# Output products and memory products as 32-row tiles, with score visits between, in a hand-ordered attention and feed-forward kernel

## The chip, the cores and the metric

The kernel runs on one core of a Trainium2 chip. The metric is the device time of one execution in microseconds (us); lower is better. A core has five engines that matter here: TensorE (PE) multiplies matrices into eight banks of PSUM, VectorE (DVE) and ScalarE (ACT) read the banks and write SBUF, GpSimd (POOL) works on SBUF alone, and SyncE (SP) issues nearly all transfers. Each engine runs its own list of instructions in order and waits on semaphores for the others.

## The reference, cut to what matters

```python
q, k, v = heads(x @ wq), heads(x @ wk), heads(x @ wv)      # 2048 tokens, D = 512, 32 heads of 16, N = 4 segments of 512
for s in range(4):                                         # one segment after the other
    p = softmax(q[s] @ k[s].T * scale + mask)              # causal inside the segment
    a_dot = p @ v[s]
    a_mem = (phi(q[s]) @ M) / (phi(q[s]) @ z + 1e-6)       # memory of the earlier segments
    o[s] = sigmoid(beta) * a_mem + (1 - sigmoid(beta)) * a_dot
    M += phi(k[s]).T @ v[s];  z += phi(k[s]).sum(tokens)
a = o @ wo
b = (relu(x @ W_gate) * (x @ W_up)) @ W_down               # F = 1792
out = g * a + (1 - g) * b                                  # g = sigmoid((x * gate_w).sum(-1))
```

Everything is bf16 in memory; `B_x` is not used.

## The kernel before, in words

All weights are loaded once and stay in SBUF, and the four segments of 512 tokens are worked through in turn. For each segment there are these stages, all issued on PE:

- **Projections** (`proj`): 12 column blocks of q, k and v, each of 4 matmuls of 128x128 by 512 columns.
- **Score visits** (`visit`, names `quad...`): the 32 heads of 16 are laid out so that four blocks of scores are made at once by matmuls on four 32-row tiles of the array (`tile_position=(32j, 0)`), one PSUM bank for each. A visit of four banks is followed by one exponential on ACT over 2048 columns (line 714). In segments 1 to 3 `SEVEN` joins seven quads into four visits of seven blocks each (four banks and three banks, two exponentials). The first segment has 18 visits, the other three 15 each: 63.
- **Masks** on POOL (line 723), and **pv** (`flush`, names `pv...`): probabilities by values, on tiles of 64 rows by 32 columns, one for each of 4 groups of heads, followed on DVE and POOL by a chain (transposes, reciprocal, products) that ends in `oT`, the attention's share of the output product.
- **Memory** (`mu`, names `mu...`, on tiles of 64 columns) and **`nd`**: for each of 4 token tiles a product `num` (4 matmuls of 128x128 by 136 columns, of which only the blocks on the diagonal are not zero), then on DVE denominators, a reciprocal and a scaled product, and a transposing DMA into `amemT`.
- **Feed-forward** (`ffn`): 14 blocks of gate and up products, relu and a product into `hT`.
- **Output products** (`outp`, names `ob...`, `oo...`): for each of the 4 token tiles 14 matmuls with `W_down` (line 876) and 4 with `wo` (line 869) add up in one bank; `fin` scales the bank into `osb` on DVE (line 884) or ACT (line 885) and `st` stores it. `between` issues `outp` and `nd` of segment s-1 and s after the first visit of segment s, so they share the time with the visits of segment s.

A PE operation is in one of four modes, by the shape of its tiles: `f` (whole array: projections, feed-forward, output products, num), `r` (32 rows: visits), `h` (pv) and `c` (mu).

Which operation comes when is not decided by the loops. `program` numbers every operation as it adds it; `ORDER` holds, for each engine, the full list of these numbers in the order in which the engine executes them, and `BANKS` one digit for each use of PSUM (an `Epoch`), its first bank. `Sched` turns both into instructions and semaphore waits: an operation waits for what it reads, for the readers of what it overwrites, and for the readers of the bank's last holder. A PE operation is usually two matmuls of one accumulation, and operations of different stages alternate.

Numbered in this way, PE's list of before changes mode 145 times. Around the output products of segment 0, for example, it reads (a bar for each change of mode, xN for N operations in a row):

```
quad | pv | proj, ob x3 | quad (7 blocks) | ob, oo x10 | quad (7) | ob, oo x8 | quad (7) | ob, oo x8 | quad (7) | ob, oo x3, num, ffn, proj, num, ffn | quad ...
```

Of the kernel before, what the change touches and what calls it, by code (L numbers as in the profile page):

```python
# [47 lines left out]
1485 1486 1487 1488""",  # L48
    "act": """
# [892 lines left out]
```

## Time and profile before

| what | value |
|---|---|
| time, three runs | 261.5, 261.03 and 261.54 us; median 261.5 us |
| span of the profiled execution (first to last instruction) | 260.0 us; about 1.5 us of the time lies outside it |
| PE busy | 252.7 us (97% of the span) |
| ACT, DVE, POOL busy | 188.0, 171.7, 121.2 us (72%, 66%, 47%) |
| granted TensorE clock | 1.000 |

The profiled execution's own time is not listed apart from the three runs, so the span and the median stand side by side. In a line of instructions or of the timeline the first number is the start in us from the span's start and the second how long the group lasted; `x4` counts instructions. The ends of matmuls are modelled, so that successive matmuls overlap in the records: what counts is the distance from start to start. A few matmul records are missing, which shows as a gap of 0.16 us "issue" or a count one short.

### The profile page before, as it was taken

The numbers are of one execution on the slowest core, as the hardware profiler recorded it, in microseconds if no ns is written. First come the engines' busy times: TensorE is split into PE (matmuls) and PEld (weight loads), VectorE is DVE, ScalarE is ACT, GpSimd is POOL, SyncE is SP. The second block draws the span as 40 slices with busy tenths as digits, with TensorE's granted clock in tenths as the row PEclk, the third lists the DMA queues.
The fourth block names the chain that finished last, engine by engine and source line by source line (L and its number), as shares of the span: only waits on it lengthen the run. The fifth ranks groups of instructions, "written<-read, shape, count | busy, mean of one in ns | idle before, by whom it ended". The sixth has DMA issues, their size and how long they took to land.

```text
span 260.0 us, 6414 instructions
## 1 busy us (share of the span) xinstructions
PE 252.7 (97%) x2621; PEld 115.4 (44%) x2655; DVE 171.7 (66%) x342; ACT 188.0 (72%) x173; POOL 121.2 (47%) x295
## 2 busy tenths in 40 slices
PE   8999999999999999999999999999999999999997
PEld 4433443434444544444544444434444445343544
DVE  2487788778655789777834478677762138875764
ACT  4598898988778788987777666979787685787000
POOL 2014766575736372587402944257620881168100
DMA  6899997115362311422041023100023022100002
GB/s 217 244 297 221 204 171 162 59 61 143 69 151 52 64 26 37 84 42 63 3 126 42 3 42 59 28 0 0 4 45 83 15 28 43 40 4 0 3 3 81
DMA packets 34925, 19.61 MB, mean 75 GB/s; under 512 B 24144, under 2 KB 34256, under 8 KB 34896
## 3 DMA queue, kind: packets, MB, share of 16 engines
q1 hardware_dynamic: 34512, 18.80, 31.5%
q8 instruction: 21, 0.34, 0.6%
q10 hardware_dynamic: 384, 0.40, 0.4%
q14 instruction: 8, 0.07, 0.1%
HBM read 10.14 MB, written 2.11 MB: 47 GB/s over the span
## 4 chain that ended last, share of the span: by engine, by line
PE 97%; issue 2%; DVE 0%
PE ps L839 38%; PE ps L876 19%; PE ps L589 11%; PE ps L703 9%; PE ps L753 7%; PE ps L587 5%; PE ps L869 5%; PE ps L646 1%; PE ps L506 1%; PE ps L629 1%; PE ps L518 0%; PE ps L527 0%; DVE osb L884 0%
## 5 line engine op out<-in xcount | busy, mean ns | idle before, releaser
L714 ACT ACTIVATE E<-ps 128x2048 bf16<-128x2048 f32 (+1 forms) x75 | 134.3, 1808 | 35.0 <-PE ps L703 34.9
L723 POOL TENSOR_SCALAR_AFFINE_SELECT E<-E 128x256 bf16<-128x256 bf16 (+1 forms) x256 | 100.9, 422 | 103.7 <-ACT E L714 90.3
L839 PE MATMUL ps<-xT,wg 128*128 128x512 bf16 x216 | 58.7, 380 | 1.1 <-issue 0.6
L839 PE MATMUL ps<-xT,wu 128*128 128x512 bf16 x213 | 57.4, 380 | 1.6 <-issue 1.6
L876 PE MATMUL ps<-wd,hT 128*128 128x512 bf16 (+2 forms) x231 | 52.7, 366 | 0.9 <-issue 0.8
L850 DVE TENSOR_TENSOR hT<-ps,rl 128x512 bf16<-128x512 f32 x56 | 37.9, 681 | 14.7 <-PE ps L839 14.2
L876 PEld LDWEIGHTS ps<-wd,hT 128*128 128x128 bf16 x238 | 21.7, 98 | 25.0 <-issue 2.5
L839 PEld LDWEIGHTS ps<-xT,wu 128*128 128x128 bf16 x224 | 20.0, 98 | 25.5 <-issue 3.9
L839 PEld LDWEIGHTS ps<-xT,wg 128*128 128x128 bf16 x224 | 20.2, 98 | 24.5 <-issue 2.8
L884 DVE TENSOR_SCALAR osb<-ps,omg 128x512 bf16<-128x512 f32 (+2 forms) x15 | 10.6, 715 | 27.9 <-PE ps L869 23.9
L703 PE MATMUL ps<-qT,kp 32*128 32x512 bf16 (+7 forms) x512 | 27.6, 286 | 0.0
L761 DVE STREAM_TRANSPOSE Tn<-ps 128x512 f32<-128x512 f32 x32 | 21.4, 699 | 8.3 <-PE ps L753 8.2
L848 DVE TENSOR_SCALAR rl<-ps 128x512 bf16<-128x512 f32 x27 | 18.3, 684 | 9.3 <-PE ps L839 9.2
L847 ACT ACTIVATE rl<-ps 128x512 bf16<-128x512 f32 x29 | 17.1, 595 | 6.7 <-PE ps L839 6.7
L703 PEld LDWEIGHTS ps<-qT,kp 32*128 32x128 bf16 x512 | 9.1, 92 | 24.9 <-ACT E L714 9.3
L753 PE MATMUL ps<-E,vaug 64*17 64x128 bf16 (+7 forms) x512 | 18.6, 283 | 0.0
L753 PE MATMUL ps<-E,vsh 64*17 64x128 bf16 (+7 forms) x512 | 18.2, 283 | 0.0
L770 POOL TENSOR_TENSOR adT<-Tn,rdg 128x512 bf16<-128x512 f32 x12 | 12.7, 1055 | 11.7 <-DVE rdg L768 8.8
L587 PE MATMUL ps<-wv,xT 128*128 128x512 bf16 x60 | 16.6, 379 | 0.6 <-issue 0.6
L589 PE MATMUL ps<-xT,wk 128*128 128x512 bf16 x62 | 16.8, 379 | 0.1
L869 PE MATMUL ps<-wo,oT 128*128 128x512 bf16 (+2 forms) x67 | 16.1, 366 | 0.1
L589 PE MATMUL ps<-xT,wq 128*128 128x512 bf16 (+2 forms) x67 | 15.9, 367 | 0.2 <-issue 0.2
(70 smaller groups left out, 215.8 us busy)
## 6 DMA issues: line engine op xcount, KB each, us to landing
vsh<-vaug SPq DMA_DIRECT2D x8, 272.0 KB, 3.2
out_dram<-osb SPq DMA_DIRECT2D x15, 128.0 KB, 1.9
wg<-in_B_W_gate_dram SPq DMA_DIRECT2D x8, 224.0 KB, 6.1
wu<-in_B_W_up_dram SPq DMA_DIRECT2D x8, 224.0 KB, 5.2
osb<-in_A_x_dram SPq DMA_DIRECT2D x14, 128.0 KB, 3.0
wd<-in_B_W_down_dram SPq DMA_DIRECT2D x7, 256.0 KB, 3.4
wk<-in_A_wk_dram SPq DMA_DIRECT2D x4, 128.0 KB, 3.6
wv<-in_A_wv_dram SPq DMA_DIRECT2D x4, 128.0 KB, 3.6
```

Of the source, the lines that this page charges most:

```text
L587: ins = e.matmul(A(ep)[:, :], lhsT=V.xT[:, kt, tok + col * 128:tok + (col + 1) * 128], rhs=w[:, kt, :], start=(kt == 0), stop=(kt == KT - 1))
L589: ins = e.matmul(A(ep)[:, c0:c1], lhsT=w[:, kt, col * 128:(col + 1) * 128], rhs=V.xT[:, kt, tok + c0:tok + c1], start=(kt == 0 and c0 == 0 ...
L703: ins = q.matmul(PS[:, ep.bank + i, o:o + w], lhsT=V.kp[r, kslot(s, G), c, :], rhs=V.qT[r, qslot(s, G), q0:q0 + w], start=True, stop=True, ...
L714: return a.activation(V.E[:, n * 512:(n + k) * 512].rearrange("q (b n) -> q b n", n=512), PS[:, x.bank:x.bank + k, :], ACT.Exp, scale=SCALE)
L723: pool(lambda g, ap=ap, lim=lim: g.affine_select(out=ap, in_=ap, compare_op=ALU.is_ge, fill=0.0, base=lim, pattern=[[0, 4], [1, 64]], chan ...
L753: ins = q.matmul(A(eps[p])[32 * jj:32 * jj + 17, 64 * (c + u):64 * (c + u + n)], lhsT=v[:, 8 * G + 2 * jj + p, :], rhs=V.E[r, f:f + 64 * n ...
L761: dve(lambda e, p=p, ep=eps[p]: e.transpose(V.Tn[:, 2 * (G % (TNN // 2)) + p, :], A(ep)[:, :]), 709, writes=[f"Tn{2 * (G % (TNN // 2)) + p ...
L839: ins = e.matmul(A(ep)[:, :], lhsT=w[:, kt, f * 128:(f + 1) * 128], rhs=V.xT[:, kt, c % XR * 512:(c % XR + 1) * 512], start=(kt == 0), sto ...
L848: ("dve", lambda e, ep=eg, r=r: e.tensor_scalar(V.rl[:, r, :], A(ep)[:, :], 0.0, None, ALU.max), t_dve(512))],
L850: dve(lambda e, ep=eu, r=r, hs=hs: e.tensor_tensor(V.hT[:, hs, :], A(ep)[:, :], V.rl[:, r, :], ALU.mult), t_dve(512), reads=[f"rl{r}"], wr ...
L869: ins = e.matmul(A(ep)[:, 0:c1 - c0], lhsT=V.oT[:, ot[G], i * 128:(i + 1) * 128], rhs=V.wo[:, G, c0:c1], start=st_ and G == 0, stop=sp_ an ...
L876: ins = e.matmul(A(ep)[:, 0:c1 - c0], lhsT=V.hT[:, slots[f], i * 128:(i + 1) * 128], rhs=V.wd[:, f, c0:c1], start=st_ and f == f0, stop=sp ...
```

## The change

- `outp` of segments 0 to 2 becomes `outr`. Every 128x128 matmul by 512 columns is cut into four of 32 rows. One operation is two rows of the contraction times four token tiles, 8 matmuls on four tiles of the array, each into its own bank. There are four phases `p`; in a phase token tile i uses row tile (i+p)%4, and the phases run over all 18 blocks of the contraction. So four banks are held from the first to the last operation of a segment's output products, and all four sums end with the last one. The first operation of phases 1 to 3 waits for PE's own last operation of the phase before. There are 36 operations for each segment, in mode `r`. Segment 3 keeps the old form.
- `nd` takes two token tiles at once: one `num` of 32 matmuls of 32x128 by 34 columns (only the blocks that aren't zero), mode `r`, over four banks; DVE then does two `nde`, one `ndr` and one new `ndg` for both tiles and two `ndm`.
- `SEVEN` is empty: all visits have four banks, 72 visits instead of 63, 72 exponentials instead of 75.
- The cost that the planner holds for `gate` and its list of names `PORT` change; they issue no instruction.
- `ORDER` and `BANKS` are new for all engines.

Numbered in the same way, the new list changes mode 139 times. 19 of the 72 visits stand inside the runs of output products, and of the six `num` one does (at the end of the run in segment 3). The runs read, with their banks:

```
segment 0's products: ob x2, quad, ob x5, quad, ob x6, quad, ob x5, quad, ob x9, quad, ob x5, quad, ob x4, quad | ffn (bank 5, after fin0_1) ...
segment 1's products: ob x3, quad, ob x5, quad, ob x5, quad, ob x5, quad, ob x9, quad, ob x5, quad, ob x4, quad | proj (bank 5, after fin1_0) ...
segment 2's products: ob x3, quad, ob x5, quad, ob x5, quad, ob x5, quad, ob x8, quad, ob x5, quad, ob x5, num | ffn (bank 6, after fin2_0) ...
ob: banks 4 to 7; every quad and the num: banks 0 to 3
```

At the start PE's list now has 30 matmuls of 512 columns and one visit ahead of the second half of `v0_1` (which needs the fourth quarter of `wv`), before 28 and none; and 52 matmuls and three visits ahead of the second half of `wu0_0` (which needs the last quarter of the first half of `W_up`), before 62 and three. SP's list there was `wv2, wv3, gwb, wg0_1, wg0_0, wg0_2, wu0_1, wg0_3, wu0_0, ldxr2, wu0_3, ldx1_2, wu0_2` and is now `wv2, gwb, wg0_1, wv3, wg0_2, wg0_0, wg0_3, wu0_0, wu0_1, ldxr2, wu0_3, ldx1_2, wu0_2`. At the very end the last token tile's two column chunks (384 and 128 wide) change places: now the 384-wide sum ends last, is scaled on ACT and stored last; before it was the 128-wide one, scaled on DVE.

```diff
-SEVEN = [(), (1,), (1,), (1,)]
+SEVEN = [(), (), (), ()]
...
     def nd(s):
-        for i in range(4):
-            ep = Epoch("mid", 2)
+        for i in (0, 2):
+            ep = Epoch("mid", 4)
...
             def fnum(e, i=i, ep=ep):
-                for G in range(4):
-                    ins = e.matmul(nv(ep)[:, 8 * G:8 * G + 8, 0:17], lhsT=V.phiq[:, G, i * 128:(i + 1) * 128], rhs=V.Mbd16[:, G, :], start=True, stop=True)
+                for u in range(2):
+                    for G in range(4):
+                        for j in range(4):
+                            r = slice(32 * j, 32 * j + 32)
+                            ins = e.matmul(nv(ep, u)[:, j, G, :, 0:17], lhsT=V.phiq[r, G, (i + u) * 128:(i + u + 1) * 128], rhs=V.Mbd16[r, G, 34 * j:34 * j + 34], start=True, stop=True,
+                                           tile_position=(32 * j, 0), skip_group_check=True)
                 return ins
...
+    def outr(s, slots):
+        ot = [(s * 4 + G) % OTN for G in range(4)]
+        eps = [Epoch("out") for _ in range(4)]
+        eps[0].group = eps
+        src = [(V.hT[:, slots[f], :], V.wd[:, f, :], f"hT{slots[f]}", f"wd{f // 2 * 2}") for f in range(NF)] + [(V.oT[:, ot[G], :], V.wo[:, G, :], f"oT{ot[G]}", f"wo{G}") for G in range(4)]
+        prev = None
+        for p in range(4):
+            for k0 in range(0, len(src), 2):
+                def fn(e, p=p, k0=k0):
+                    for k in (k0, k0 + 1):
+                        for i in range(4):
+                            j = (i + p) % 4
+                            r = slice(32 * j, 32 * j + 32)
+                            ins = e.matmul(A(eps[i])[:, :], lhsT=src[k][0][r, i * 128:(i + 1) * 128], rhs=src[k][1][r, :], start=p == 0 and k == 0, stop=p == 3 and k == len(src) - 1,
+                                           tile_position=(32 * j, 0), skip_group_check=True)
+                    return ins
+                x = pe(fn, mm(512, 2), reads=[y for k in (k0, k0 + 1) for y in src[k][2:]], writes=[y.res for y in eps[1:]], name=f"ob{s}_{p}_{k0}", ep=eps[0], role="w" if p == 0 and k0 == 0 else "w2", mode="r")
+                if p and k0 == 0:
+                    x.preds.append((prev, False))
+                prev = x
+        for i in range(4):
+            fin(s, i, eps[i], 0, 512, False)
```

More of the change, by code (lines that the diff above doesn't have):

```diff
@@ L97, in t_pool @@
     return 160.0 + 0.975 * n * rate
-PORT = ("kmask", "qts", "kts", "qphi", "kphi", "rdg", "ad", "oa", "gate", "omg1", "vone", "romgh", "epsv", "pmb")
+PORT = ("kmask", "qts", "kts", "qphi", "kphi", "rdg", "ndg", "ad", "oa", "gate", "omg1", "vone", "romgh", "epsv", "pmb")
 class Res:
@@ L549, in program @@
             dve(lambda e, t=t, row=row: e.tensor_tensor_reduce(out=row, in0=row, in1=V.gwb[:], scale=1.0, scalar=0.0, op0=ALU.mult, op1=ALU.add, accum_out=V.gl[:, t:t + 1]),
-                                 900, reads=rows + ["gwb"], writes=rows + [f"gl{t}"], name=f"gate{t}")
+                                 740, reads=rows + ["gwb"], writes=rows + [f"gl{t}"], name=f"gate{t}")
         act(lambda e, t0=t0, t1=t1, gx=gx: e.activation(gx, V.gl[:, t0:t1], ACT.Exp), 197, reads=[f"gl{t}" for t in range(t0, t1)], writes=[f"gexp{c}"], name="gexp")
@@ L640, in nd, with nv @@
     def nd(s):
-        for i in range(4):
-            ep = Epoch("mid", 2)
+        for i in (0, 2):
+            ep = Epoch("mid", 4)
+            def nv(ep, u):
+                return A(ep)[:, :, 256 * u:256 * u + 256].rearrange("q j (g h c) -> q j g h c", g=4, c=32)
             def fnum(e, i=i, ep=ep):
-                for G in range(4):
-                    ins = e.matmul(nv(ep)[:, 8 * G:8 * G + 8, 0:17], lhsT=V.phiq[:, G, i * 128:(i + 1) * 128], rhs=V.Mbd16[:, G, :], start=True, stop=True)
-                return ins
-            def nv(ep):
-                return A(ep).rearrange("q b (h c) -> q (b h) c", c=32)
-            pe(fnum, mm(136, 4) + 17.0, reads=[f"phiq{G}" for G in range(4)] + [f"Mbd16_{j}" for j in range(4)], name=f"num{s}_{i}", ep=ep, role="w")
-            rd = V.rdm[:, 32 * i:32 * i + 32]
-            dve(lambda e, ep=ep, rd=rd: e.tensor_tensor(rd, nv(ep)[:, :, 16], V.epsv[:, :], ALU.add), 195, reads=["epsv"], writes=[f"rdm{i}"], name=f"nde{s}_{i}", ep=ep, role="r")
-            dve(lambda e, i=i: e.reciprocal(V.rdm[:, 32 * i:32 * i + 32], V.rdm[:, 32 * i:32 * i + 32]), 352, reads=[f"rdm{i}"], writes=[f"rdm{i}"], name=f"ndr{s}_{i}")
-            dve(lambda e, i=i, ep=ep, rd=rd: e.scalar_tensor_tensor(V.amem[:, i % 2, :].rearrange("q (h c) -> q h c", c=16), nv(ep)[:, :, 0:16], V.gexp[:, 4 * s + i:4 * s + i + 1],
-                                                                             rd.unsqueeze(2).to_broadcast([128, 32, 16]), op0=ALU.mult, op1=ALU.mult),
-                          745, reads=[f"rdm{i}", f"gexp{s}"], writes=[f"amem{i % 2}"], name=f"ndm{s}_{i}", ep=ep, role="r")
-            dma("sp", lambda e, i=i: e.dma_start_transpose(V.amemT[:, :, i * 128:(i + 1) * 128], V.amem[:, i % 2, :]), 1 << 17, occ=1280.0, reads=[f"amem{i % 2}"], writes=[f"amemT{i}"], name=f"aT{s}_{i}")
@@ new lines, in fnum @@
+                for u in range(2):
[4 more added lines that the diff above has]
+                                           tile_position=(32 * j, 0), skip_group_check=True)
+                return ins
+            pe(fnum, 212.0, reads=[f"phiq{G}" for G in range(4)] + [f"Mbd16_{j}" for j in range(4)], name=f"num{s}_{i}", ep=ep, role="w", mode="r")
@@ new lines, in nd @@
+            rds = V.rdm[:, 32 * i:32 * i + 64]
+            for u in range(2):
+                dve(lambda e, ep=ep, rds=rds, u=u: e.tensor_tensor(rds[:, 32 * u:32 * u + 32].rearrange("q (j g h) -> q j g h", g=4, h=2), nv(ep, u)[:, :, :, :, 16],
+                                                                   V.epsv[:, :].rearrange("q (g j h) -> q j g h", g=4, h=2), ALU.add), 186,
+                    reads=["epsv"], writes=[f"rdm{i + u}"], name=f"nde{s}_{i + u}", ep=ep, role="r")
+            dve(lambda e, rds=rds: e.reciprocal(rds, rds), 545, reads=[f"rdm{i}", f"rdm{i + 1}"], writes=[f"rdm{i}", f"rdm{i + 1}"], name=f"ndr{s}_{i}")
@@ new lines, in nd @@
+            dve(lambda e, rds=rds, t=4 * s + i: e.tensor_tensor(rds.rearrange("q (u m) -> q u m", u=2), rds.rearrange("q (u m) -> q u m", u=2), V.gexp[:, t:t + 2].unsqueeze(2).to_broadcast([128, 2, 32]), ALU.mult), 225,
+                reads=[f"rdm{i}", f"rdm{i + 1}", f"gexp{s}"], writes=[f"rdm{i}", f"rdm{i + 1}"], name=f"ndg{s}_{i}")
+            for u in range(2):
+                rd = rds[:, 32 * u:32 * u + 32].rearrange("q (j g h) -> q j g h", g=4, h=2)
+                dve(lambda e, t=(i + u) % 2, u=u, ep=ep, rd=rd: e.tensor_tensor(V.amem[:, t, :].rearrange("q (g j h c) -> q j g h c", g=4, h=2, c=16), nv(ep, u)[:, :, :, :, 0:16],
+                                                                                rd.unsqueeze(4).to_broadcast([128, 4, 4, 2, 16]), ALU.mult),
+                    690, reads=[f"rdm{i + u}"], writes=[f"amem{(i + u) % 2}"], name=f"ndm{s}_{i + u}", ep=ep, role="r")
+                dma("sp", lambda e, i=i + u: e.dma_start_transpose(V.amemT[:, :, i * 128:(i + 1) * 128], V.amem[:, i % 2, :]), 1 << 17, occ=1280.0, reads=[f"amem{(i + u) % 2}"], writes=[f"amemT{i + u}"], name=f"aT{s}_{i + u}")
@@ L851, in ffn, with fin @@
         return slots
+    def fin(s, i, ep, c0, c1, last):
+        t, w = 4 * s + i, c1 - c0
+        r = t % 3 if last else t % 2
+        om = V.omg[:, t:t + 1]
+        res = [f"osb{r}_0", f"osb{r}_1"] if w == 512 else [f"osb{r}_{c0 // 384}"]
+        sc.add(Op([("dve", lambda e: e.tensor_scalar(V.osb[:, r, c0:c1], A(ep)[:, 0:w], om, None, ALU.mult), t_dve(w) + 60.0),
+                   ("act", lambda e: e.activation(V.osb[:, r, c0:c1], A(ep)[:, 0:w], ACT.Copy, scale=om), t_act(w, True, 1))][:1 if w == 128 else 2],
+                  reads=[f"omg{s}"], writes=res, name=f"fin{s}_{i}", ep=ep, role="r"))
+        dma("sp", lambda e: e.dma_start(out[0, t * 128:(t + 1) * 128, c0:c1], V.osb[:, r, c0:c1]), w * 256, reads=res, writes=[f"out{t}_{c0}"], name=f"st{t}")
@@ L853, in outp @@
     def outp(s, slots):
+        if s < NSEG - 1:
+            return outr(s, slots)
         ot = [(s * 4 + G) % OTN for G in range(4)]
         for i in range(4):
-            t = 4 * s + i
-            for c0, c1 in (((0, 512),) if t < NT - 1 else ((0, 384), (384, 512))):
+            for c0, c1 in (((0, 512),) if i < 3 else ((0, 384), (384, 512))):
                 ep = Epoch("out")
                 w = c1 - c0
-                last = s == NSEG - 1
-                order = ["d"] * (NF // 2) + ["o"]
-                f0 = 0
-                for ci, kind in enumerate(order):
-                    st_, sp_ = ci == 0, ci == len(order) - 1
-                    if kind == "o":
-                        def fa(e, i=i, ep=ep, c0=c0, c1=c1, st_=st_, sp_=sp_):
-                            for G in range(4):
-                                ins = e.matmul(A(ep)[:, 0:c1 - c0], lhsT=V.oT[:, ot[G], i * 128:(i + 1) * 128], rhs=V.wo[:, G, c0:c1], start=st_ and G == 0, stop=sp_ and G == 3)
-                            return ins
-                        rd = [f"oT{ot[G]}" for G in range(4)] + [f"wo{G}" for G in range(4)]
-                        pe(fa, mm(w, 4), reads=rd, name=f"oo{s}_{i}", ep=ep, role="w" if st_ else "w2")
-                    else:
-                        def fb(e, i=i, ep=ep, f0=f0, c0=c0, c1=c1, st_=st_, sp_=sp_):
-                            for f in (f0, f0 + 1):
-                                ins = e.matmul(A(ep)[:, 0:c1 - c0], lhsT=V.hT[:, slots[f], i * 128:(i + 1) * 128], rhs=V.wd[:, f, c0:c1], start=st_ and f == f0, stop=sp_ and f == f0 + 1)
-                            return ins
-                        rd = [f"hT{slots[f]}" for f in (f0, f0 + 1)]
-                        pe(fb, mm(w, 2), reads=rd + [f"wd{f0}"], name=f"ob{s}_{i}_{f0}", ep=ep, role="w" if st_ else "w2")
-                        f0 += 2
-                r = t % 3 if last else t % 2
-                om = V.omg[:, t:t + 1]
-                res = [f"osb{r}_0", f"osb{r}_1"] if w == 512 else [f"osb{r}_{c0 // 384}"]
-                sc.add(Op([("dve", lambda e, ep=ep, r=r, om=om, c0=c0, c1=c1: e.tensor_scalar(V.osb[:, r, c0:c1], A(ep)[:, 0:c1 - c0], om, None, ALU.mult), t_dve(w) + 60.0),
-                                      ("act", lambda e, ep=ep, r=r, om=om, c0=c0, c1=c1: e.activation(V.osb[:, r, c0:c1], A(ep)[:, 0:c1 - c0], ACT.Copy, scale=om), t_act(w, True, 1))][:1 if w == 128 else 2],
-                                     reads=[f"omg{s}"], writes=res, name=f"fin{s}_{i}", ep=ep, role="r"))
-                dma("sp", lambda e, r=r, t=t, c0=c0, c1=c1: e.dma_start(out[0, t * 128:(t + 1) * 128, c0:c1], V.osb[:, r, c0:c1]), w * 256,
-                               reads=res, writes=[f"out{t}_{c0}"], name=f"st{t}")
@@ new lines, in outp, with fb @@
+                for f0 in range(0, NF, 2):
+                    def fb(e, i=i, ep=ep, f0=f0, c0=c0, c1=c1):
+                        for f in (f0, f0 + 1):
+                            ins = e.matmul(A(ep)[:, 0:c1 - c0], lhsT=V.hT[:, slots[f], i * 128:(i + 1) * 128], rhs=V.wd[:, f, c0:c1], start=f == 0, stop=False)
+                        return ins
+                    pe(fb, mm(w, 2), reads=[f"hT{slots[f]}" for f in (f0, f0 + 1)] + [f"wd{f0}"], name=f"ob{s}_{i}_{f0}", ep=ep, role="w2" if f0 else "w")
@@ L890, in program, with fa @@
+                def fa(e, i=i, ep=ep, c0=c0, c1=c1):
+                    for G in range(4):
+                        ins = e.matmul(A(ep)[:, 0:c1 - c0], lhsT=V.oT[:, ot[G], i * 128:(i + 1) * 128], rhs=V.wo[:, G, c0:c1], start=False, stop=G == 3)
+                    return ins
+                pe(fa, mm(w, 4), reads=[f"oT{ot[G]}" for G in range(4)] + [f"wo{G}" for G in range(4)], name=f"oo{s}_{i}", ep=ep, role="w2")
+                fin(s, i, ep, c0, c1, True)
     proj(0)
```

16 lines of the change are left out of this document (8 added, 8 removed), and 83 rows, old and new, of the table ORDER.

## The prediction

> **What bounds the kernel now.** I read the page first (busy shares, then the chain that ended last), then the groups of instructions, then short pieces of the timeline of PE, ACT, DVE and SP.
>
> ```profile
> span 260.0 us, 6414 instructions
> PE 252.7 (97%) x2621; PEld 115.4 (44%) x2655; DVE 171.7 (66%) x342; ACT 188.0 (72%) x173; POOL 121.2 (47%) x295
> ...
> PE 97%; issue 2%; DVE 0%
> ```
>
> The chain is PE from end to end; no other engine holds a visible share. So the time is what PE streams, what it pays for changing mode, and where it stands. Prices of the first two, from PE's timeline, with its first projection and its last group:
>
> ```profile
> 4.87 0.92 PE L589 MATMUL ps<-xT,wq 128*128 128x384 bf16 x6
> ...
> 257.73 0.39 PE L869 MATMUL ps<-wo,oT 128*128 128x128 bf16 x4
> ...
> 81.39 0.42 PE L646 MATMUL ps<-Mbd,phiq 128*128 128x136 bf16 x4
> 81.64 1.03 PE L839 MATMUL ps<-xT,wg 128*128 128x512 bf16 x4
> 82.50 1.03 PE L589 MATMUL ps<-xT,wk 128*128 128x512 bf16 x4
> 83.37 0.42 PE L646 MATMUL ps<-Mbd,phiq 128*128 128x136 bf16 x4
> 83.62 1.03 PE L839 MATMUL ps<-xT,wg 128*128 128x512 bf16 x4
> 84.58 0.40 PE L703 MATMUL ps<-qT,kp 32*128 32x512 bf16 x4
> 84.91 0.39 PE L839 MATMUL ps<-xT,wg 128*128 128x512 bf16 x1
> ...
> 64.62 0.61 PE L703 MATMUL ps<-qT,kp 32*128 32x448 bf16 x14
> 65.17 2.76 PE L876 MATMUL ps<-wd,hT 128*128 128x512 bf16 x12
> ...
> 47.63 0.70 PE L629 MATMUL ps<-vaug,phik 128*64 128x68 bf16 x32
> 48.26 0.39 PE L753 MATMUL ps<-E,vaug 64*17 64x512 bf16 x4
> ```
>
> Read starts, not durations. Eight full matmuls take 83.37-81.64 = 1.73, so 0.216 each. Four matmuls and a visit take 84.91-83.62 = 1.29; less five passes of 0.216 that leaves 0.21 for two changes of mode, 0.105 each (the four matmuls of a visit make one pass, side by side). A seven-block visit lasts 0.55 to the next start against 0.33 for a four-block one: a second pass costs 0.22. A `num` costs 0.25.
>
> By the program's counts that gives 237.0 us of streaming (projections 41.4, feed-forward 96.7, output products 62.2, scores 16.2, pv 16.0, num 3.0, mu 1.5) and 145 x 0.105 = 15.2 of changes. With the first projection at 4.87 it makes 257.1; PE's stream ends at about 257.9, just behind the start of its last group. So PE stands less than 1 us in all, most of it among the first loads. Any wait that the change brings is paid in full.
>
> **The change, part by part: what PE saves.**
>
> - Changes of mode, 145 to 139: 6 x 0.105 = -0.6. It is so few because nine more visits and five lone num, in a mode that their neighbours don't have, take back most of what 19 visits inside the runs save.
> - Score passes: 63 visits with 75 passes become 72 with 72: 3 x 0.216 = -0.65.
> - `num`: 12 x 0.25 = 3.0 become 6 of 8 passes of 34 columns, a shape the trace lacks. The 32 matmuls of `mu` take 0.63 less one change, 0.52, at two side by side, so 0.033 a pass; 8 of them 0.26, 6 num 1.6: -1.4. If four tiles don't help, 0.52 each: 0. I take -1.4, as visits do run four side by side.
> - Output products: 3 x 72 matmuls become 3 x 72 passes of four. The second pass of a visit (0.22) is nearest: 0 to +0.8; I take 0. Visits don't accumulate, these do: a rival below.
>
> Sum -2.7. Of the rest of the step that changes nothing is on the chain: DVE does as many `nde` and `ndm`, two `ndr` and two `ndg` in place of four `ndr` for each segment; ACT three exponentials fewer; SP issues as many stores and transposing transfers.
>
> **What PE waits for in the runs.** The eight banks are now full: four results, four for the visit. The rows that set each wait:
>
> ```profile
> 85.03 1.88 ACT L714 ACTIVATE E<-ps 128x2048 bf16<-128x2048 f32 x1 [0.86 <-PE ps L703]
> ...
> 67.77 1.03 PE L869 MATMUL ps<-wo,oT 128*128 128x512 bf16 x4
> 68.84 0.75 DVE L884 TENSOR_SCALAR osb<-ps,omg 128x512 bf16<-128x512 f32 x1 [0.83 <-PE ps L869]
> ...
> L885 ACT ACTIVATE osb<-ps,omg 128x512 bf16<-128x512 f32 x2 | 1.4, 690 | 0.2 <-PE ps L869 0.2
> ...
> 3.95 0.41 PE L527 MATMUL ps<-ident,hT 128*128 128x128 bf16 x4
> ...
> hT<-in_A_x_dram ACTq DMA_DIRECT2D x1, 256.0 KB, 3.0
> ...
> 0.86 0.40 ACTq L450 DMA_DIRECT2D hT<-in_A_x_dram  x1
> ```
>
> A visit at 84.58 has its exponential from 85.03 (0.45 later) to 86.91. Release to matmul: hT lands at 0.86+3.0 = 3.86 to 3.9 and PE starts at 3.95, so 0.05 to 0.09. The same four banks can be visited again after 0.45+1.88+0.05 = 2.38 to 2.42.
>
> - A visit and five operations (10 passes) take 11 x 0.216 = 2.38: nine such intervals, 0 to 0.04 each: +0.2.
> - The last visit of the first two runs comes after only four operations, 1.94: it stands 0.44, twice +0.9.
> - After it PE goes on with work for a result bank, which `fin` must free. DVE starts 68.84-68.42 = 0.42 after the start of the last matmul (67.77 + 3 x 0.216) and takes 0.75; with the release 1.22 to 1.26, and 1.0 after the stream's end. Of that the visit, its wait and the change fill 0.44+0.22+0.105 = 0.76: +0.27, twice. In the third run fin is ACT's (0.42+0.69+0.07-0.22 = 0.97), and num and a change fill 0.36: +0.6. Together +1.1. What is queued behind is all of PE's list, and DVE and ACT run dry behind it.
> - The wait for PE's own last operation: a full matmul lasts 0.38 to 0.39 in the records (the last of the rows at 84.91), then 0.05 to 0.09 to the next start: 0.45 in place of 0.216, so 0.23. Of nine phase borders five have a visit between (0.216 covers it); four don't: +0.9.
>
> Sum +3.1 (2.7 without the small ones, 3.4 with the longer releases). Evictions that hid behind 18 matmuls of the next token tile have lost that cover; that is where the gain goes.
>
> **The head.** PE starts on loads that land just ahead of it:
>
> ```profile
> 13.51 0.59 PE L587 MATMUL ps<-wv,xT 128*128 128x512 bf16 x2
> 14.13 1.02 PE L839 MATMUL ps<-xT,wg 128*128 128x512 bf16 x4
> ...
> 5.99 0.91 SPq L450 DMA_DIRECT2D wv<-in_A_wv_dram  x2
> 6.93 0.43 SPq L450 DMA_DIRECT2D gwb<-in_gate_w_dram  x1
> 7.41 1.38 SPq L450 DMA_DIRECT2D wg<-in_B_W_gate_dram  x3
> ...
> wg<-in_B_W_gate_dram SPq DMA_DIRECT2D x3, 224.0 KB, 6.2
> ...
> gwb<-in_gate_w_dram SPq DMA_DIRECT2D x1, 128.0 KB, 5.9
> ...
> DMA to landing us min/median/max: 3.5/3.6/4.2
> ...
> 13.44 0.57 SPq L450 DMA_DIRECT2D wu<-in_B_W_up_dram  x1
> ...
> wu<-in_B_W_up_dram SPq DMA_DIRECT2D x1, 224.0 KB, 5.0
> ```
>
> (The 3.5/3.6/4.2 are those of wv.) The fourth wv, issued at 6.46, lands at 10.66. Now it is issued third, behind gwb and the first wg, near 7.41. PE comes to it after 30 matmuls and a visit, 4.87 + 30 x 0.216 + 0.43 = 11.8. With its own 4.2 it lands at 11.6 and nothing is lost. But transfers land in the order of issue, gwb at 12.8 and the wg issued at 7.41 (with 5.9 to 6.2) at 13.3 to 13.6; the same three transfers in another order are all in by then, wv last. So PE stands 0 to 1.7. A second bound: the last wu, at an unchanged place, lands at 13.44+5.0 = 18.4, and PE wants it after 52 matmuls and three visits, at 17.4: 1.0 at least, in all. The 0.2 that PE stands now (two matmuls from 13.51 end at 13.94, next at 14.13) falls away. I take 1.5-0.2 = +1.3, nearer the row of the place than wv's own.
>
> **The tail.**
>
> ```profile
> L884 DVE TENSOR_SCALAR osb<-ps,omg 128x128 bf16<-128x128 f32 x1 | 0.3, 350 | 0.3 <-PE ps L869 0.3
> ...
> out_dram<-osb SPq DMA_DIRECT2D x1, 96.0 KB, 1.7
> ...
> out_dram<-osb SPq DMA_DIRECT2D x1, 32.0 KB, 1.5
> ```
>
> The last eviction is 384 wide on ACT; by 690 ns for 512 it takes some 0.58 in place of 0.35, and its 96 KB land 0.2 later: +0.4.
>
> **Sum.** -2.7+3.1+1.3+0.4 = +2.1: a span of 262.1. The median of the runs is 1.5 above the profiled span, so the forecast is 261.5+2.1 = **263.6 us**.
>
> **A rule against this.** The Trainium skill, "TensorE: Matmul & The Clock Gate", section "Measured speedup vs the span model", gives 3.07x, not 4x, for four row tiles of 32 by 512 columns. By it 216 passes of 0.216 grow by 0.30 of 46.7, +14.1, where the second pass of a visit above gives at most +0.8; no run so far accumulates on four row tiles.
>
> **The rivals.**
>
> - *The loads come in time* (for the head's +1.3 a gain of 0.2, and 0.2 of the stands before 4.87 with it, since the first transposes change places): the fourth wv needs 4.2 as before, and the last wu comes a us sooner. The median of wv speaks for it, the order of landings against. It decides from wv by 11.7 and wu by 17.3. -2.7+3.1-0.4+0.4 = +0.4: 261.9, not measurably slower; with the waits at their lower end (2.7) and passes as they are, 261.2 to 261.5, and if releases inside a run without changes of mode are a tenth shorter at each of its stands, 260.7.
> - *Four tiles don't accumulate side by side:* if one pass in each four tiles has to be made again, 216 x 0.072 = +15.6 on the forecast, 279. The passes of visits, which write four banks at once, speak against it.
> - *Further waits.* Behind each run something else may end last:
>
> ```profile
> L655 DVE SCALAR_TENSOR_TENSOR amem<-ps,gexp,rdm 128x512 bf16<-128x512 f32 x12 | 8.8, 747 | 0.2
> ...
> L654 DVE RECIPROCAL rdm<-rdm 128x32 f32<-128x32 f32 x12 | 4.2, 351 | 0.3
> ...
> L653 DVE TENSOR_TENSOR rdm<-ps,epsv 128x32 f32<-128x32 f32 x12 | 2.0, 184 | 6.8 <-PE ps L646 6.7
> ...
> out_dram<-osb SPq DMA_DIRECT2D x15, 128.0 KB, 1.9
> ```
>
> A num now holds four banks until its second `ndm`: 0.2 to the start, three small operations of 0.18 (the new `ndg` too), a reciprocal of 0.35 to 0.70 and two products of 0.75, 2.6 to 3.0; PE has seven to nine operations or a pv there, 3.0 to 4. And the four `fin` come at once into two `osb` rows, so the third waits for the first one's store (0.75+1.9); it frees the bank that the next pv takes, 4.3 after the run. Both fit, narrowly; masks on POOL may also be late for a pv. One that doesn't fit costs 0.5 to 2: 264 to 266.
>
> **How the numbers follow.** Chances: the forecast 0.54, loads in time 0.30, further waits 0.12, tiles not side by side 0.04. About 0.2% (0.5 us) can be told from no change. The forecast and the waits are slower (0.66, less 0.02 at their lower end); loads in time spreads over 260.7 to 262.3: 0.14 faster, 0.13 same, 0.03 slower. Together faster 0.14, same 0.15, slower 0.71. The range runs from 261.0, which leaves out the faster cases, to 265.2 (num at its upper end +1.4, or a late pv); the forecast's own is 262.4 to 264.9.
>
> **What would show it.** Starts of successive passes in the runs at 0.216 to 0.22, and num groups near 0.26. Four stands of 0.23 at phase borders, 0.44 ahead of the last visit of two runs, and after each run a start 1.0 behind its last pass, released by fin. In the head a stand ahead of v's second half until 13.4, released by a transfer. 139 changes. The prediction is wrong if the head doesn't stand, if passes take more than 0.22, or if PE is released sooner than a record's end and 0.05.

## The result, and the profile after

The changed kernel takes 263.37 us (median of five runs, 263.06 to 263.58) against 261.4 us (261.03 to 261.54) for the kernel before: a ratio of 1.0071, 95% interval 1.0056 to 1.0086. Taken again beside later experiments it was 262.97 us, ratio 1.0059 (1.0041 to 1.0078). So it is slower by 1.5 to 2 us, as forecast (263.6). The profiled execution took 263.41 us, 1.2 more than its span. In every execution whose time and span are both on record, of both kernels, the time lies about 1.2 above the span, not 1.5: the span of 260.0 before goes with an execution of about 261.2 us, not with the median of 261.5.

The page of the changed kernel: span, PE's row, the shares of the chain.

```profile
span 262.2 us, 8006 instructions
PE 256.4 (98%) x3447; PEld 114.3 (44%) x3447; DVE 169.5 (65%) x338; ACT 191.7 (73%) x174; POOL 119.6 (46%) x295
...
PE 91%; DMA 3%; SPq 2%; DVE 1%; ACT 0%; issue 0%
```

PE is still the bound. Its busy share can't be compared with the one before: there the records of 34 of 2655 matmuls are missing (the page counts 2621 matmuls and 2655 weight loads), here none, and e1 below, this kernel but for one load's place, misses 32 and shows 252.0 us. New on the chain are DMA and SP's queue with 5%: by line about 4% is the head (SP's issues and the transfer of wv) and 1% a store. The rest is in PE's timeline, in three pieces: a phase border (start of segment 0's products), the end of that run, and the end of segment 2's run.

```profile
64.48 1.04 PE L888 MATMUL ps<-wd,hT 32*128 32x512 bf16 x16
65.36 0.39 PE L715 MATMUL ps<-qT,kp 32*128 32x448 bf16 x8
65.57 2.33 PE L888 MATMUL ps<-wd,hT 32*128 32x512 bf16 x40
67.74 0.40 PE L715 MATMUL ps<-qT,kp 32*128 32x320 bf16 x8
67.97 1.03 PE L888 MATMUL ps<-wo,oT 32*128 32x512 bf16 x16
69.09 1.91 PE L888 MATMUL ps<-wd,hT 32*128 32x512 bf16 x32
70.82 0.39 PE L715 MATMUL ps<-qT,kp 32*128 32x384 bf16 x8
...
80.83 1.03 PE L888 MATMUL ps<-wo,oT 32*128 32x512 bf16 x16
82.12 0.40 PE L715 MATMUL ps<-qT,kp 32*128 32x320 bf16 x8 [0.26 <-ACT E L726]
82.73 1.04 PE L851 MATMUL ps<-xT,wg 128*128 128x512 bf16 x4 [0.20 <-DVE osb L870]
83.60 1.03 PE L590 MATMUL ps<-xT,wk 128*128 128x512 bf16 x4
84.56 0.37 PE L653 MATMUL ps<-Mbd,phiq 32*128 32x34 bf16 x32
84.87 1.47 PE L851 MATMUL ps<-xT,wg 128*128 128x512 bf16 x6
...
209.37 0.41 PE L653 MATMUL ps<-Mbd,phiq 32*128 32x34 bf16 x32
210.33 1.90 PE L851 MATMUL ps<-xT,wg 128*128 128x512 bf16 x8 [0.55 <-ACT osb L871]
...
212.92 1.47 PE L851 MATMUL ps<-xT,wu 128*128 128x512 bf16 x6
214.66 0.39 PE L765 MATMUL ps<-E,vaug 64*17 64x512 bf16 x4 [0.28 <-DVE osb L870]
```

Read starts again. 32 small matmuls take 70.82-69.09 = 1.73 us: 0.216 for four, the price of one full matmul, though each four accumulate into four banks. Four passes from 67.97 should end at 68.83; the next phase starts at 69.09: 0.26 for PE's own last operation. Nothing is marked there, since the record of that last matmul lasts nearly until the wait is over. The last visit should start at 80.83+4 x 0.216 = 81.69 and starts at 82.12: 0.43, released by the exponential. After it, 82.12+0.216+0.105 = 82.44 against 82.73: 0.29, released by `fin`. In the third run 209.37+0.2+0.105 = 209.68 against 210.33: 0.65. A `num` costs 84.87-84.56 less a change, 0.2. The bracketed idle is smaller than these stands, because it counts from the modelled end of the record before and not from where the next pass could have begun.

The head, in the timeline of PE and of SP's queue:

```profile
4.05 0.85 PE L528 MATMUL ps<-ident,hT 128*128 128x128 bf16 x6
4.69 0.42 PE L519 MATMUL ps<-ident,hT 128*128 128x128 bf16 x2
...
12.15 0.59 PE L590 MATMUL ps<-xT,wk 128*128 128x512 bf16 x2
13.11 1.47 PE L588 MATMUL ps<-wv,xT 128*128 128x512 bf16 x6 [0.36 <-DMA wv<-in_A_wv_dram]
...
7.41 0.43 SPq L451 DMA_DIRECT2D wv<-in_A_wv_dram  x1
```

and the landing of the wv loads, from the view of that tile:

```profile
DMA to landing us min/median/max: 3.4/3.6/5.7
```

The fourth wv is issued at 7.41 and takes 5.7 in place of 4.2 us; PE is released at 13.11. But it stands only 13.11-12.15-0.43 = 0.53 there, since it came 0.8 late itself: six matmuls of 128 columns from 4.05 to 4.69 take 0.107 each, twice the full-rate 0.055. That half rate lasted until 6.0 us here; in the profile before it ended between 3.7 and 4.0, where PE stood for a load.

The tail, PE's last group and the last eviction:

```profile
258.99 0.81 PE L915 MATMUL ps<-wo,oT 128*128 128x384 bf16 x4
259.84 0.58 ACT L871 ACTIVATE osb<-ps,omg 128x384 bf16<-128x384 f32 x1 [2.79 <-PE ps L915]
```

PE's stream ends at 258.99+4 x 0.1625 = 259.64, 2.56 before the end of the span; before it was 257.73+4 x 0.056 = 257.95 and 2.05.

### The profile page after: what moved, and what is told of

It reads as the page before. It is cut to its first block, busy times and chain, and to the rows that moved or that the text cites. A ratio compares the mean times of both kernels' runs of the same rounds, so it can differ in the third digit from the quotient of the medians.

```text
span 262.2 us, 8006 instructions
## 1 busy us (share of the span) xinstructions
PE 256.4 (98%) x3447; PEld 114.3 (44%) x3447; DVE 169.5 (65%) x338; ACT 191.7 (73%) x174; POOL 119.6 (46%) x295
## 4 chain that ended last, share of the span: by engine, by line
PE 91%; DMA 3%; SPq 2%; DVE 1%; ACT 0%; issue 0%
PE ps L851 37%; PE ps L888 18%; PE ps L590 9%; PE ps L715 8%; PE ps L765 7%; PE ps L588 5%; PE ps L909 5%; SPq L451 2%; DMA wv<-in_A_wv_dram 2%; PE ps L915 1%; DVE osb L870 1%; DMA out_dram<-osb 1%; PE ps L630 1%; PE ps L653 1%; ACT osb L871 0%
## 5 line engine op out<-in xcount | busy, mean ns | idle before, releaser
L726 ACT ACTIVATE E<-ps 128x2048 bf16<-128x2048 f32 x72 | 135.1, 1876 | 36.7 <-PE ps L715 36.1
L735 POOL TENSOR_SCALAR_AFFINE_SELECT E<-E 64x256 bf16<-64x256 bf16 (+1 forms) x256 | 99.8, 419 | 110.2 <-ACT E L726 95.7
L851 PE MATMUL ps<-xT,wu 128*128 128x512 bf16 x224 | 58.6, 380 | 0.0
L888 PE MATMUL ps<-wd,hT 32*128 32x512 bf16 x672 | 39.9, 375 | 0.3
L715 PE MATMUL ps<-qT,kp 32*128 32x192 bf16 (+7 forms) x512 | 28.4, 286 | 0.5 <-ACT E L726 0.5
L888 PEld LDWEIGHTS ps<-wd,hT 32*128 32x128 bf16 x672 | 15.9, 93 | 18.9 <-PE ps L888 2.3
L590 PE MATMUL ps<-xT,wk 128*128 128x512 bf16 x64 | 17.6, 380 | 0.0
L590 PE MATMUL ps<-xT,wq 128*128 128x512 bf16 (+2 forms) x68 | 17.5, 373 | 0.0
L870 DVE TENSOR_SCALAR osb<-ps,omg 128x512 bf16<-128x512 f32 (+1 forms) x10 | 6.7, 706 | 16.3 <-PE ps L888 11.7
L871 ACT ACTIVATE osb<-ps,omg 128x512 bf16<-128x512 f32 (+1 forms) x7 | 4.6, 671 | 15.6 <-PE ps L915 15.4
```

Of the source, the lines that this page charges most:

```text
L590: ins = e.matmul(A(ep)[:, c0:c1], lhsT=w[:, kt, col * 128:(col + 1) * 128], rhs=V.xT[:, kt, tok + c0:tok + c1], start=(kt == 0 and c0 == 0 ...
L715: ins = q.matmul(PS[:, ep.bank + i, o:o + w], lhsT=V.kp[r, kslot(s, G), c, :], rhs=V.qT[r, qslot(s, G), q0:q0 + w], start=True, stop=True, ...
L726: return a.activation(V.E[:, n * 512:(n + k) * 512].rearrange("q (b n) -> q b n", n=512), PS[:, x.bank:x.bank + k, :], ACT.Exp, scale=SCALE)
L735: pool(lambda g, ap=ap, lim=lim: g.affine_select(out=ap, in_=ap, compare_op=ALU.is_ge, fill=0.0, base=lim, pattern=[[0, 4], [1, 64]], chan ...
L851: ins = e.matmul(A(ep)[:, :], lhsT=w[:, kt, f * 128:(f + 1) * 128], rhs=V.xT[:, kt, c % XR * 512:(c % XR + 1) * 512], start=(kt == 0), sto ...
L888: ins = e.matmul(A(eps[i])[:, :], lhsT=src[k][0][r, i * 128:(i + 1) * 128], rhs=src[k][1][r, :], start=p == 0 and k == 0, stop=p == 3 and ...
```

## The experiments

The theory: the sum of the prediction. The rivals: that the small matmuls themselves cost more than full ones; that the head's loss is not wv's place; that the tail is a fixed time. The times of the variants of the changed kernel other than e5 and e6 lie within 0.3% of each other, with intervals of about 0.2% to either side (e3 is of the kernel before), so these are told apart by their traces. Two starts in each trace measure them: that of the first run (64.48 after) closes the head, and from there to the first of the last `wo` groups (255.31 after) lies everything else but the tail.

| run | ratio to before, 95% | median us | first run starts | from there to the last wo groups |
|---|---|---|---|---|
| changed kernel | 1.0071 (1.0056 to 1.0086) | 263.37 | 64.48 | 190.83 |
| e9, the same again | 1.0059 (1.0041 to 1.0078) | 262.97 | 64.21 | 190.48 |
| e1 early wv | 1.0047 (1.0030 to 1.0064) | 262.79 | 64.45 | 190.49 |
| e2 and longer warm-up | 1.0054 (1.0037 to 1.0071) | 263.0 | 63.97 | 190.86 |
| e4 tail | 1.0054 (1.0037 to 1.0071) | 262.9 | 64.62 | 190.48 |
| e5 full array | 1.0145 (1.0125 to 1.0165) | 265.59 | 64.19 | 192.86 |
| e6 same tiles | 1.0003 (0.9990 to 1.0016) | 261.8 | 64.36 | 189.33 |
| e7 three rows | 1.0050 (1.0033 to 1.0066) | 263.12 | 65.56 | 190.49 |
| e8 combined | 1.0045 (1.0029 to 1.0061) | 262.91 | 64.12 | 190.48 |
| e10 table first | 1.0059 (1.0042 to 1.0075) | 262.98 | 64.56 | 190.67 |
| e11 wv and k copy | 1.0045 (1.0030 to 1.0060) | 262.65 | 64.26 | 190.48 |
| e12 all head and tail | 1.0061 (1.0039 to 1.0084) | 262.76 | 64.53 | 190.48 |

**e6: the wait at the phase borders, taken away.**

```diff
-                            j = (i + p) % 4
+                            j = i
-                if p and k0 == 0:
-                    x.preds.append((prev, False))
```

> The changed kernel without the rotation of row tiles: in every phase token tile i stays on row tile i, so that a phase repeats the products of the first and three quarters of the sum over k are left out; PE then needs no wait for its own last operation at the phase borders. The number of matmuls, their shapes and their order are unchanged. Theory (that wait costs 0.25 at the four borders without a visit and 0.02 to 0.03 at the five with one): 1.1 us less, 262.2 to 262.4 us. Rival (the stand is the cost of a bank changing its row tile or of what follows in the order, and goes elsewhere): 263.2 to 263.5 us.

Measured: ratio 1.0003, 0.56% or 1.5 us under e9; from the first run on 189.33 against 190.48, 1.15 less. PE's rows of e6 at the border shown above:

```profile
67.63 0.40 PE L715 MATMUL ps<-qT,kp 32*128 32x320 bf16 x8
67.85 1.03 PE L887 MATMUL ps<-wo,oT 32*128 32x512 bf16 x16
68.72 1.90 PE L887 MATMUL ps<-wd,hT 32*128 32x512 bf16 x32
```

68.72-67.85 = 0.87, four passes and nothing more. The other stands are where they were (0.43 and 0.29 after the first two runs, 0.66 after the third). The term is shown, at 1.15 us: a quarter us each at four borders, and 0.02 to 0.03 at each of the other five. The remaining 0.35 of the 1.5 us between the medians lies within their intervals. e6 takes away the rotation of the row tiles together with the wait; that the wait is the price and not the rotation is argued from those five borders, where the tiles change too and a visit covers the wait. Without the term the rest of the change would cost about as much as it saves.

**e5: full-array matmuls at the same places.**

```diff
-                        for i in range(4):
-                            j = (i + p) % 4
...
-                            ins = e.matmul(A(eps[i])[:, :], lhsT=src[k][0][r, i * 128:(i + 1) * 128], ...
+                        ins = e.matmul(A(eps[p])[:, :], lhsT=src[k][0][:, p * 128:(p + 1) * 128], ...
```

> The changed kernel with the output products of segments 0 to 2 as full 128x128 matmuls again, at the same places in PE's order with the same score visits between them: phase p makes token tile p alone, with no wait at the phase borders, and its eviction can start after its phase. Theory (a pass of four row tiles costs what a full matmul costs; the run's price is waits, its saving the changes of mode): 36 more changes x 0.105 = +3.8, the waits at the phase borders go (-1.1), the evictions of the first three tiles are done before the run ends (-1.2 and -0.3 at a later pv), the two stands ahead of a last visit halve (-0.4): +0.8, 264.2 us (263.8 to 264.8). Rival (row-tile passes themselves are the dearer ones, by 0.01 us or more each): 216 passes save 2 us or more, 262.2 us or below.

Measured: 265.59 us, by the ratios 2.3 above e9 and 1.9 above the first runs of the changed kernel, where 0.8 was expected; the rival is out. The waits of PE between 64 and 220 us in e5 (us in total, times, longest):

```profile
PE ps L715 <- ACT E L726: 0.3, 2, 0.2
PE ps L715 <- DVE amem L667: 0.3, 1, 0.3
PE ps L765 <- DVE osb L870: 0.3, 1, 0.3
PE ps L653 <- ACT E L726: 0.2, 1, 0.2
```

and PE's rows behind the first run:

```profile
82.67 0.40 PE L715 MATMUL ps<-qT,kp 32*128 32x320 bf16 x8 [0.15 <-ACT E L726]
83.00 1.04 PE L851 MATMUL ps<-xT,wg 128*128 128x512 bf16 x4
83.87 1.03 PE L590 MATMUL ps<-xT,wk 128*128 128x512 bf16 x4
85.05 0.37 PE L653 MATMUL ps<-Mbd,phiq 32*128 32x34 bf16 x32
```

`fin` no longer releases anything behind the first run (83.00-82.67 is a visit and a change), but with nothing in front of it the `num` at 85.05 comes too early for its banks: 0.21, twice, a visit in the third run 0.36, the start of the second run 0.09. From the first run on, against the changed kernel: changes +3.85 (36 x 0.107), borders -1.13, evictions -1.15, last visits -0.44, these new stands +0.87: +2.0, measured 192.86-190.83 = 2.03. What is left for 216 passes is 0.03 us, less than these readings resolve: four row tiles cost what a full matmul costs. The expectation had missed the new stands, and the stand of the pv (0.3 in the waits above), which stayed. The Trainium skill, "TensorE: Matmul & The Clock Gate", section "Measured speedup vs the span model", has 3.07x for that shape; by an estimate from that figure the 216 passes would have been 14 us dearer. This trace does not agree: 0.216 against 0.216 is a factor of 4.

**e3: only the place of the fourth wv, in the kernel before.**

```diff
-... 17 18 27 20 ...      SP: wv, wv, gwb, wg
+... 17 27 20 18 ...      SP: wv, gwb, wg, wv
```

> The kernel before, with only this piece of the change: the fourth wv load is issued third, behind gwb and the first wg. Theory (landing by place in the issue order): wv lands near 13.1 in place of 10.62, PE comes to it at 10.92 and stands 2.1 us, of which 0.35 is given back where PE stood on wg and wu before: +1.7 us, 263.1 us. Rival (the transfer takes its own 4.2 us wherever it is issued): it lands at 11.6, +0.3 us, 261.7 us.

Measured: ratio 1.0079 (1.0050 to 1.0108), median 263.18. PE's rows of e3:

```profile
10.54 0.59 PE L589 MATMUL ps<-xT,wk 128*128 128x512 bf16 x2
12.37 0.60 PE L587 MATMUL ps<-wv,xT 128*128 128x512 bf16 x2 [1.24 <-DMA wv<-in_A_wv_dram]
```

and its wv landings:

```profile
DMA to landing us min/median/max: 3.1/3.5/4.9
```

Two places back in the queue cost that transfer 1.7 us of landing (12.33 in place of 10.62); its own 4.2 from the new issue would have given 11.6. The stand is 12.37-10.54-0.43 = 1.40, the span grows by 1.3. The place decides: wv lands behind gwb (11.45) and the wg (11.98), as the prediction took it, but the last of the three lands a us sooner than its 13.3 to 13.6.

**e1, e11: the place put back in the changed kernel, and then DVE's order.**

```diff
-... 17 27 20 18 21 ...   SP: wv, gwb, wg, wv, wg
+... 17 18 27 20 21 ...   e1 and e11
-... 95 176 ...           DVE: gate product 2, copy of k
+... 176 95 ...           e11 alone
```

> The changed kernel with the fourth wv load issued ahead of gwb and the first wg again, as before the change; nothing else differs. Theory (a transfer's place in the issue order sets when it lands, and 0.53 us of the head's loss is the stand on that wv): wv lands near 10.6 in place of 13.06, the stand ahead of v's second half at 13.11 goes, and PE runs 0.5 us ahead from there until the last wu (18.07) holds it for up to 0.3: 0.2 to 0.5 us less, 262.9 to 263.2 us. Rival (the head's loss is the first load, the late full clock and the loads' total, and wv's place only decides where PE stands): the stand moves to a wg or wu, 263.4 us.

> The kernel of e1_wv_early, in which PE's lead of 0.40 was lost again at a wg operation (17.8 us) that waited for a copy of k on DVE, itself queued behind a gate product that waited for an osb load (16.47). Here DVE makes that copy ahead of the gate product. Theory (the queue on DVE took the lead): the stand goes, PE keeps 0.3 to 0.45 us until the last wu (landing 18.1 to 18.3) becomes the bound: 0.3 to 0.45 us below e9_again, 262.6 to 262.8 us. Rival (another load takes the lead as well): within 0.15 us of e9_again.

Measured: 262.79 and 262.65 us. In e1 v's second half starts at 12.71, 0.40 sooner; but the first run starts at 64.45 against 64.48. PE's only wait in e1 between 9 and 20 us:

```profile
PE ps L851 <- DVE kT L605: 0.2, 1, 0.2
```

and DVE's rows ahead of it:

```profile
12.60 0.69 DVE L550 CUSTOM_DVE_ANT_0 hT<-hT,gwb 128x512 bf16<-128x512 bf16 x1 [0.30 <-DMA gwb<-in_gate_w_dram]
...
16.47 0.69 DVE L550 CUSTOM_DVE_ANT_0 osb<-osb,gwb 128x512 bf16<-128x512 bf16 x1 [1.02 <-DMA osb<-in_A_x_dram]
17.09 0.69 DVE L605 CAST kT<-ps 128x512 bf16<-128x512 f32 x1
```

The gate product waits for its row, and the copy that frees PE's bank stands behind it in DVE's order. So e1's theory fell and its rival held: the stand moved, to DVE's queue. With that copy ahead (e11) PE has no stand at all after 9 us; its first run starts at 64.26, 0.05 behind e9: its half rate lasted until 6.5 us, and PE comes to v's second half at 12.86, 0.03 later than in e9.

**e2, e10: the cold start.**

```diff
-    for m, n, role in ((5, 512, "w"), (4, 128, "w2")):
+    for m, n, role in ((5, 512, "w"), (8, 128, "w2")):     e2, on e1
-6 7 3 72 ...             ACT: two loads, table load, copies
+3 6 7 72 ...             e10
```

> The kernel of e1_wv_early, with eight 128-column warm-up matmuls in place of four, so that PE is not idle when hT lands (3.6 us). Theory: the full clock comes near 4 us as in the kernel before, not near 6, and PE reaches the projections 0.5 us sooner; but then the last wu (landing 18.07) holds it, so only 0.1 to 0.2 us of that is kept: 262.7 to 263.1 us. Rival (the cold start is the larger part of the head's loss and nothing else bounds it): a further 0.5 us or more below e1_wv_early, 262.4 us. If the clock comes near 6 us whatever the warm-up: equal to e1_wv_early or up to 0.2 above it.

> The changed kernel with ACT's first instructions in the order of the kernel before: the table load ahead of its two load issues. Theory (the load that is issued first lands first: the change let ACT's hT overtake SP's): SP's first hT lands at 3.26 in place of 3.6 to 3.9 and PE's transposes start 0.3 us sooner; but the fourth wv still lands near 13, PE stands there longer, and nothing is gained: 0 to 0.2 us below e9_again. Rival (the late start is the head's loss): 0.3 to 0.6 us below e9_again.

Measured: 263.0 and 262.98. In e10 the first hT lands at 3.23 and PE starts at 3.36 as before the change; yet half rate lasts until 6.4, and v's second half starts at 13.19, released by wv. With the table load first ACT issues its own load 0.05 behind SP's (0.86 against 0.81), else just ahead of it (0.80); SP's lands at 3.1 to 3.3 in four traces with the table first, at 3.6 to 3.9 in ten without, and ahead of ACT's in all of them. That is worth nothing here. In e2 PE is busy from 0.84 on, and half rate lasts until 5.4. Its span after the first run holds a stand of 0.36 at 153.6 that no other run has. PE's and ACT's rows of e2 there:

```profile
153.59 0.60 PE L851 MATMUL ps<-xT,wg 128*128 128x512 bf16 x2 [0.18 <-ACT osb L871]
...
152.85 0.69 ACT L871 ACTIVATE osb<-ps,omg 128x512 bf16<-128x512 f32 x1 [0.53 <-DMA out_dram<-osb]
```

An eviction of the second run waits for a store to leave its `osb` row and frees PE's bank late; in e9 the same eviction starts at 152.45 without a wait.

**e4: the tail.**

```diff
-... 1499 1500 1489 1490  PE: 128-column sum last operations, then 384
+... 1489 1490 1499 1500
-... 1502 1492            SP: their stores
+... 1492 1502
```

> The changed kernel with the last token tile's two sums finished the other way round: the last operations of the 384-column sum ahead of those of the 128-column sum, and their stores likewise. Theory (the tail's price is the last eviction and its store): the last eviction is 128 wide on DVE, 0.35 in place of 0.58 us, and the last store 32 KB, 0.2 us sooner: 0.2 to 0.45 us less, 262.95 to 263.2 us. Rival (the tail is a fixed time behind PE's last matmul): 263.4 us.

Measured: 262.9 us, within the interval of e9. PE's stream ends at 259.43 in e4, 2.47 before the end of its span (2.56 after the change). The rows of its end:

```profile
259.21 0.39 PE L915 MATMUL ps<-wo,oT 128*128 128x128 bf16 x4
259.30 0.58 ACT L871 ACTIVATE osb<-ps,omg 128x384 bf16<-128x384 f32 x1 [2.45 <-PE ps L915]
259.64 0.35 DVE L870 TENSOR_SCALAR osb<-ps,omg 128x128 bf16<-128x128 f32 x1 [0.56 <-PE ps L915]
```

ACT ends at 259.88, only 0.11 ahead of DVE; the 96 KB store is issued at 259.91 and takes SP 0.42, so the 32 KB one goes at 260.33 and lands at 261.88. The expectation left SP's queue out. In the kernel before, the store of the 384 columns went out at 257.91, 0.62 ahead of the last one.

**e7: a third row for segment 2's evictions.**

```diff
-        r = t % 3 if last else t % 2
+        r = t % 3 if last or s == 2 else t % 2
```

> The changed kernel with three osb rows instead of two for the evictions of segment 2, so that the third eviction does not wait for the first one's store. Theory (the 0.33 us stand of a pv at 214.66 comes from that store): the stand goes, 0.3 us less, 263.05 us. Rival (something else ends just behind it there, such as the pv's masks): 263.3 us.

Measured: 263.12 us. The stand of the pv is gone, and its cause in the changed kernel is a row of DVE:

```profile
213.20 1.41 DVE L870 TENSOR_SCALAR osb<-ps,omg 128x512 bf16<-128x512 f32 x2 [0.86 <-DMA out_dram<-osb]
```

But e9, e1 and e4, with two rows, don't show it either (190.48 to 190.49 against 190.83), nor does e6; e10 has 0.19 of it, and e2 a stand of the same kind behind the second run, where e7 has two rows as well. Whether such a store lands in time changes from one execution to the next, and the experiment can't say what a third row is worth. e7's profiled execution was its slowest, with stands of 0.21 at a pv (37.9) and 0.47 at a `mu` (49.1) that e9 lacks.

**e8, e9, e12: together, and the control.** e8 is e1, e4 and e7 in one; e12 is e10, e11 and e4; e9 is the changed kernel.

> The changed kernel with the early wv, the 128-column sum last and three osb rows together. Theory (three separate terms, at three places on PE's path): the sum of the three, 0.7 to 1.2 us less, 262.2 to 262.7 us, still above the kernel before (261.4). Rival (PE's later waits take up what is gained earlier): 262.9 us or more.

> The changed kernel once more, unaltered, as the measure for the three beside it. If the 0.33 us stand of a pv at 214.66 belongs to the kernel, it is there again and the time is 263.4 us; if it belongs to the one execution that was profiled (e1, e4 and e6 kept its two osb rows and did not show it), it is gone and the span is 0.3 us shorter, 263.0 to 263.2 us.

> The changed kernel with the table load first on ACT, the early wv, the copy of k ahead of the gate product on DVE and the 128-column sum last. Theory: the head is bounded by the last wu and gains 0.4 to 0.5 us, the tail 0.3 to 0.45 us: 0.7 to 0.95 us below e9_again, 262.2 to 262.5 us, still above the kernel before, since the waits inside the runs (3.1 us) against the saving (2.7 to 2.8 us) stay. Rival (head and tail are most of what separates the kernels): 261.6 us or below.

Measured: 262.91, 262.97 and 262.76 us. Neither sum came: the rival of e8 held. In e12 PE comes to v's second half at 12.17, nearly a us ahead of the changed kernel, and loses it at once:

```profile
13.56 0.40 PE L715 MATMUL ps<-qT,kp 32*128 32x448 bf16 x8
14.82 0.39 PE L590 MATMUL ps<-xT,wk 128*128 128x512 bf16 x1 [0.86 <-DVE vaug L618]
...
13.06 0.69 DVE L550 CUSTOM_DVE_ANT_0 hT<-hT,gwb 128x512 bf16<-128x512 bf16 x1 [1.29 <-DMA gwb<-in_gate_w_dram]
```

Here gwb landed at 13.03, and the copy of v that frees the bank stands behind the first gate product. Three bounds lie within a us of each other in this head (the fourth wv, the gate's loads through DVE's queue, the clock), and lifting one shows the next. No variant here beats the kernel before.

## Why the prediction was right, step by step

| term | forecast | measured |
|---|---|---|
| changes of mode, score passes, num | -2.7 | -2.9, a remainder: PE's end (+1.69) less the stands and the head below |
| five-operation intervals | +0.2 | 0; no visit there is late by 0.02 |
| last visit after four operations | +0.9 | 0.43 + 0.43 |
| `fin` behind the runs | +1.1 | 0.28 + 0.28 + 0.65 = 1.21 |
| PE's own last operation | +0.9 | 1.01 at four borders, 0.12 at the five covered ones; e6: 1.15 |
| a pv behind an eviction behind a store | none in the sum, a rival | 0.33 in this execution, 0 in e9 |
| head | +1.3 | +1.1: 13.11 against the forecast's 11.8, less the 0.2 that fell away |
| tail | +0.4 | 2.56 - 2.05 = +0.5 |
| span | +2.1 | +2.2 |

- *Savings.* Passes of four row tiles at 0.216 as taken; e5 shows it to 0.03 us over all of them. The one mis-sized piece is `num`, 0.2 in place of 0.26 (-0.36): four tiles of 34 columns fit better than the step from `mu` let expect.
- *Waits in the runs.* All three kinds stood at the forecast places with the forecast releasers and within 0.05 each. The estimate of 0.23 for PE's own operation, from a record's length and a release, measured 0.244 to 0.254. The five covered borders cost 0.02 to 0.03 each and not nothing; the small +0.2 for the five-operation intervals did not come.
- *The head.* Its size was right, its cause only half, so the size was in part luck. The late wv was there, and e3 shows its price alone. But the forecast let PE arrive at 11.8, by the clock of the one profile before; it arrived at 12.58. Over seven traces with the late wv v's second half starts at 12.8 to 13.5, and it makes little difference whether PE is held by the clock (e9: a stand of 0.05) or by the load (e4: 1.2). With the wv early it starts at 12.2 to 12.9, and in three of those five DVE's queue takes the lead back (e1, e8, e12). The step that fell short is that it named two bounds of the head, wv and the last wu, and no third: the gate products ahead of the copies on DVE that free PE's banks were not looked at, and the last wu bound only once (e12, 0.05).
- *Further waits.* The rival's third `fin`, waiting for a store, did come, in some executions, at 0.2 to 0.4 us (e10, the changed kernel, e2); "Both fit, narrowly" was fair. It moved the profiled time by 0.3, not by the 0.5 to 2 that the rival named.
- *The tail* came as forecast, but e4 shows that the eviction's width is not its cause alone; the stores' issue on one queue holds the end as well.
- *The step from the span to the time.* 1.5 us was taken, 1.2 is what each execution shows. The forecast of 263.6 has this 0.3 too much; its span of 262.1 is the fairer one to compare, and 262.2 came.

## What to carry to other kernels

When work with its own eviction is spread over all banks at once, count what it stops hiding: each of these three runs saved about 1 us of mode changes and passes and paid about 1 us of waits, because results that had been evicted behind the next tile now all end together. A PE that never stands before a change makes such waits easy to forecast: start of the last pass, plus the releaser's latency and length, less what PE has to do meanwhile. A head bounded by loads can't be mended one load at a time; list what every engine's queue holds behind each late transfer before moving one.

## What the runs showed of the hardware

- The half rate of PE's start lasts a different time in each execution. By the spacing of its starts it ended at 3.5 us (e3) and between 3.7 and 4.0 (before) in the two profiles in the order of the kernel before, and between 4.5 (e8) and 6.5 us (e11) in twelve of the changed kernel and its variants, e10 and e12 with the same first start of PE (3.36) among them. The Trainium skill, "TensorE: Matmul & The Clock Gate", section "What's actually happening", says that the activity window runs free of the kernel's start and that the change of rate therefore moves by half a us either way; no trace here shows that window, and the change of rate moves by more than that here, over a range of 2 us. Whether the order before really comes to full rate sooner, or two early draws were luck, is open.
- A bank that goes from one row tile to another behind a wait for PE's own last matmul costs 0.244 to 0.254 us (the changed kernel and e9 against e6), unless other work of one pass (0.216) lies between; then 0.02 to 0.03.
- From the first run to the last groups seven executions (e1, e4, e7, e8, e9, e11, e12) agree to 0.01 us: 190.48 to 190.49. Nearly all that scatters in these traces lies in the head and in one store.
